# A spectral mix and a gated MLP on one core: the last down products of half 0 moved among the chains of half 1, row additions of half 0 alternating with half 1's rows, six fewer stored low parts

## Chip, cores and metric

One NeuronCore of one Trainium2 chip. The metric is the device time in microseconds of the kernel; three runs of the kernel before took 1344.32, 1346.24 and 1347.97 us, median 1346.24.

## What is computed

```python
g = sigmoid((x * gate_w).sum(-1, keepdims=True))
a = irfft2(rfft2(x) * (w_r + 1j * w_i), s=(S, D))     # S = 2048 tokens, D = 576
h = gelu(xB @ w_gate) * (xB @ w_up)                   # 576 -> 4608; here xB is A_x
b = h @ w_down                                        # 4608 -> 576
return g * a + (1 - g) * b
```

All in float32. The two branches share x. A float32 operand is kept as a high part rounded to 12 bits and a low part, the rest; a product takes three matmuls: high by high, low by high, high by low.

## The kernel before

**TensorE's programme.** The MLP sets the order. The tokens are two halves of 1024, p = 0 and 1, and a half runs over all 36 column blocks of the hidden layer, two at a time (18 pairs i). A step is numbered j = 36p + 2i, so step NT = 36 is the first of half 1. The first FIRST[p] pairs (3 and 7) are done by `normal`: for each of two token tiles tb, `hidden` runs a chain of 14 matmuls (128x512, `chain`) for the gate, one for the up weights, then gelu and the product, and splits the result into a buffer hb, hx, ext or part of gub. The other pairs are done by `products`: a block of seven products in place of eight (a11, a12, s2, s3, s1, a22, s4; n = 0 to 6), each two runs of seven matmuls (`seven`), from sums and differences of the weights (`prep`) and of the tokens (kept in til, xhi, xlo). Results wait in a list `pend`; `down` pops one: 12 matmuls of 128x288 (L909) into one of two PSUM banks pdn, evicted by ScalarE into one of four buffers stg (L941), and added to the output in DRAM, yd, by a DMA that accumulates, issued on GpSimd's queue, here Pool (L922).

**The other engines' order.** Every engine works strictly in the order in which the program issues to it. `gap()` is called twice in a chain, once after a run of seven, once after a down product; it counts, and issues what has come due: `at(n, fn)` runs fn n gaps later, `aux` holds one thing for each gap, `seq` a chain of steps with their distances, and `due` forces the rest of one when its result is needed. What is left of VectorE's time goes to a generator, `spectral`, by a credit: a matmul adds RATE times its time, an operation of the MLP subtracts its cost, and the spectral work (transforms along the rows in the tile rows, along the columns in til) continues while the credit is above zero.

**Between the halves.** In the last block of half 0, `leave(n)` loads the weights of step NT (early, in tmp) and the tokens of half 1 (rows), makes the hi and lo tokens of tile 0, and at n = 5 the high part of step NT's weights and the first of four loads til<-away (L1334), due 1, 6, 18 and 26 gaps later, for the column transforms. At n = 6 it issues the load of step NT+1 (L777, L778, into low) and queues the tokens of tile 1. Then six down products run (two of hb and hx, four of ext and gub), with the loads and copies of further weights between them (`prep_gu`, `prep_dn`: ScalarE copies the high part, VectorE subtracts, `lower` at L802), and then the first chain of half 1, step 36.

**The rows back.** `inverse_rows(h)` spreads half h's spectrum over rows (L545, L548, ScalarE L240), runs the row transforms, and adds each of the eight row tiles, scaled by the gate (L648 on ScalarE for odd t of half 0, else L650 on VectorE), to yd by an accumulating DMA (L651). A place for the scaled tile is one of three (part of gub, two spare), in turn; in half 1 four more in tmp. Half 1's spectrum lies in DRAM, spilt[0] and spilt[1], and passes through tmp (L636, L625).

**Low parts.** `lows`: for j of 14 to 35, the low part of w_down is stored to DRAM in half 0 (L805, SyncE) and loaded in half 1 (L798, Pool), so that VectorE need not subtract again.

Of the kernel before, what the change touches and what calls it, by code (L numbers as in the profile page):

```python
# [15 lines left out]
P = 128  # L16
S = 2048
D = 576
# [157 lines left out]
def _build(nc, tc, a):  # L176
    with ExitStack() as ctx:
# [376 lines left out]
        def waits(n):  # L554
            for _ in range(n):
                yield None
# [47 lines left out]
        def inverse_rows(h):  # L604
            pl.memset(rows.rearrange("p (c k) -> p c k", c=2)[:, :, 8 * KF:], 0.0)
            if h == 0:
                for e in range(2):
                    nc.sync.dma_start(spilt[e], til[:, 4 * SW * (2 + e):4 * SW * (3 + e)])
                fourth = [ext[:, 0:TB], ext[:, TB:2 * TB], xraw[:, 1]]
                for i in range(3):  # L610
                    nc.sync.dma_start(fourth[i], four_d[:, TB * i:TB * (i + 1)])
                T = til[:, 0:8 * SW].rearrange("p (t c k) -> p t c k", t=8, c=2)
                yield from moved(lambda t, c: (spread(c, t), T[:, t, c, 0:KF]), range(7, -1, -1))
                parts, tails = set_operands()
                for n in range(3):
                    nc.sync.dma_start(f(tails[3 + n]), kept[3 + n])
                for n in (1, 2, 0):
                    nc.sync.dma_start(f(parts[n].rearrange("p l t k -> p (l t k)")), kept[n][:, 0:2048])
                    nc.sync.dma_start(f(tails[n]), kept[n][:, 2048:])
                ops["ready"] = 1  # L620
                yield from inverse_stages()
            else:
                for e in range(2):
                    if e:
                        nc.sync.dma_start(tmp[:, 0:4 * SW], spilt[e])  # L625
                        yield from waits(9)
                    yield from moved(lambda t, c: (spread(c, t), batch[:, t - 4 * e, c, 0:KF]),
                                     range(4 * e, 4 * e + 4))
                yield from inverse_stages()
            R = rows.rearrange("p (k t) -> p t k", t=8)  # L630
            todo_t = list(range(8))
            while ops.get("phase") != 1:
                yield None
            places = [zb[0][:, 1920:1920 + D]] + spare
            if h == 0:
                at(2, lambda: nc.sync.dma_start(tmp[:, 0:4 * SW], spilt[0]))  # L636
            else:
                places += [tmp[:, D * i:D * (i + 1)] for i in range(4)]
            n = count[0]
            while todo_t:  # L640
                if count[0] >= n:
                    t = min(todo_t, key=lambda t: abs(count[0] - added[8 * h + t] - 11)) if h else todo_t[0]
                    todo_t.remove(t)
                    u = 8 * h + t
                    o = places.pop(0)
                    places.append(o)
                    if h == 0 and t % 2:
                        act.activation(o, R[:, t, 0:D], AF.Copy, scale=gs[:, u:u + 1])  # L648
                    else:
                        vec.tensor_scalar(o, R[:, t, 0:D], gs[:, u:u + 1], None, op0=ALU.mult)  # L650
                    at(2, lambda u=u, o=o: pl.dma_start(yd[u], o, accum_op=ALU.add))  # L651
                    n = count[0] + 1 + len(todo_t) % 2
                    yield 0.8
                else:
                    yield None
            yield from waits(3)
            ops["half"] = h + 1

        def load_rows(h):
            nc.sync.dma_start(rows[:, 0:8 * D], a["xn"][h])  # L660
# [129 lines left out]
            while q:  # L790
                q.pop(0)()

        lows = {j: dram.tile([P, D], F32, name=f"lo{j}", tag=f"lo{j}") for j in range(2 * FIRST[1], NT)}

        def lower(key, g, r, cost):
            j, kept_low = key[1], lows.get(key[1] % NT) if key[0] == "dn" else None
# [425 lines left out]
        def products(b, i):  # L1222
# [42 lines left out]
            for n, (name, nd) in enumerate(zip(("a11", "a12", "s2", "s3", "s1", "a22", "s4"), downs)):  # L1265
                m = n + 3
                b.prep(i + m // 7, m % 7)
                if n == 0 and i > b.first:
                    b.load_d(i)
                if p and n in (3, 4):  # L1270
# [41 lines left out]
        def leave(n):  # L1312
            nonlocal til

            if n == 0:
                assert ops["kept"]
                load_w(NT)
                for k in range(KT):
                    nc.sync.dma_start(rows[:, TB * k:TB * (k + 1)], a["xt"][1][:, k, 0:TB])
            if n == 2:  # L1320
                for k in range(KT):
                    aux.append(lambda k=k: prep_x(0, k, rows[:, TB * k:TB * (k + 1)]))
            if n == 1:
                for k in range(KT):
                    nc.sync.dma_start(rows[:, TB * (KT + k):TB * (KT + k + 1)], a["xt"][1][:, k, TB:2 * TB])
            if n == 5:
                z = BLOCKS[0][2]
                gub[z] = mk(f"gub{z}", [2560], F32R)
                prep_gu(NT)
            if n == 5:  # L1330
                til = mk("til", [16 * SW])
                there, here = (x.rearrange("p (e d k) -> p d e k", d=4, e=4) for x in (away, til))
                for d, n in enumerate((1, 6, 18, 26)):
                    at(n, lambda d=d: nc.sync.dma_start(here[:, d], there[:, d]))  # L1334
# [87 lines left out]
        def normal(p, i, tb, b):  # L1422

            j = 2 * (p * NBLK + i)
            first, last = p == 0 and i == 0, i == b.first - 1
            if last and tb == 0:
# [15 lines left out]
            def mid():  # L1442
                for _ in range(2):
                    if pend:
                        down(*pend.pop(0))

            if last and tb == 1:
                b.prep(b.first, 2, 4)
# [15 lines left out]
        for p in range(2):  # L1464
# [22 lines left out]


# [54 lines left out]
```

## Time and profile before

| | |
|---|---|
| median of three runs | 1346.24 us |
| the profiled execution | 1349.53 us, span 1347.8 us, mean granted TensorE clock 0.998 |
| TensorE busy | 1330.0 us |
| VectorE, ScalarE, GpSimd busy | 1141.1, 834.9, 274.9 us |
| DMA | 253.61 MB |
| TensorE idle in 640 to 700 us (60 us) | 4.57 us |
| in 900 to 1000 and 1000 to 1200 us | 1.42 and 1.83 us |

A row of a timeline gives the start and the duration in us, engine, line, operation and operands (out<-in, with partitions x elements), and in brackets the idle time ahead of it with what ended it. PE is TensorE, DVE VectorE, ACT ScalarE, SP SyncE; SPq marks the queue on which a DMA was issued. In a window's row stand its length, then the busy time of PE, weight loads, VectorE, ScalarE and GpSimd, the granted clock, the DMA share and GB/s. A row of the DMA issues gives the size and the median us from issue to landing. The span runs from the first to the last instruction; the time of an execution holds a little more.

### The profile page before, as it was taken

The numbers are of one execution on the slowest core, as the hardware profiler recorded it, in microseconds if no ns is written. First come the engines' busy times: TensorE is split into PE (matmuls) and PEld (weight loads), VectorE is DVE, ScalarE is ACT, GpSimd is POOL, SyncE is SP. The second block draws the span as 40 slices with busy tenths as digits, with TensorE's granted clock in tenths as the row PEclk, the third lists the DMA queues.
The fourth block names the chain that finished last, engine by engine and source line by source line (L and its number), as shares of the span: only waits on it lengthen the run. The fifth ranks groups of instructions, "written<-read, shape, count | busy, mean of one in ns | idle before, by whom it ended". The sixth has DMA issues, their size and how long they took to land.

```text
span 1347.8 us, 20213 instructions
## 1 busy us (share of the span) xinstructions
PE 1330.0 (99%) x7322; PEld 1173.3 (87%) x7322; DVE 1141.1 (85%) x1610; ACT 834.9 (62%) x1484; POOL 274.9 (20%) x350
## 2 busy tenths in 40 slices
PE   9999999999999999999899999999999999999998
PEld 7888888888888888888788888888888888888888
DVE  6999998789999988765688877879999948999964
ACT  5557656666665675786456666634675667666652
POOL 0021112212221221122201222111122232222241
PEclk9999999999999999999999999999999999999999
DMA  8464677787677679998979999767767799777797
GB/s 307 158 142 107 127 130 162 173 222 145 144 154 149 139 182 249 237 269 222 267 236 232 243 250 244 156 137 230 226 145 150 152 191 220 142 148 148 169 218 203
DMA packets 114755, 253.61 MB, mean 188 GB/s; under 512 B 13792, under 2 KB 24032, under 8 KB 112864
## 3 DMA queue, kind: packets, MB, share of 16 engines
q0 software_dynamic: 46880, 98.00, 44.2%
q1 hardware_dynamic: 67776, 154.34, 34.5%
q8 instruction: 57, 0.93, 0.3%
q14 instruction: 42, 0.34, 0.1%
HBM read 134.01 MB, written 111.13 MB: 182 GB/s over the span
## 4 chain that ended last, share of the span: by engine, by line
PE 84%; DVE 5%; DMA 3%; ACT 2%; issue 1%; POOL 0%; DVEq 0%; SPq 0%; ACTq 0%
PE pdn L909 29%; PE pgu L1216 18%; PE px L1216 17%; PE pgu L1218 3%; PE px L1218 3%; PE pgu L830 3%; PE pgu L831 3%; PE pgu L832 3%; PE px L302 1%; DMA low<-wd 1%; DMA yd<-spare 1%; PE px L830 1%; PE px L831 1%; PE px L832 1%; PE pgu L836 1%
## 5 line engine op out<-in xcount | busy, mean ns | idle before, releaser
L922 POOL DMA_DIRECT2D yd<-stg x264 | 225.2, 855 | 977.1 <-ACT stg L941 826.6
L941 ACT ACTIVATE stg<-pdn,omg 128x576 f32<-128x576 f32 x276 | 204.3, 741 | 307.9 <-PE pdn L909 197.7
L909 PE MATMUL pdn<-dn,hb 128*128 128x288 f32 x1644 | 241.6, 294 | 2.3 <-ACT stg L941 2.2
L909 PEld LDWEIGHTS pdn<-dn,hb 128*128 128x128 f32 x1644 | 231.7, 188 | 12.1 <-ACT stg L941 2.8
L240 ACT ACTIVATE gub<-low 128x512 fp32r<-128x512 f32 (+3 forms) x138 | 96.2, 697 | 37.9 <-DVE low L1193 19.5
L1216 PE MATMUL pgu<-xhi,gub 128*128 128x512 f32 x376 | 116.9, 392 | 0.9 <-ACT px L240 0.9
L1203 DVE TENSOR_TENSOR gub<-low,gub 128x768 fp32r<-128x768 f32 x114 | 108.5, 952 | 10.3 <-PE px L1218 6.5
L909 PE MATMUL pdn<-dn,ext 128*128 128x288 f32 x624 | 100.2, 296 | 5.1 <-ACT stg L941 4.6
L1216 PE MATMUL pgu<-til,gub 128*128 128x512 f32 x396 | 101.3, 391 | 0.0
L909 PEld LDWEIGHTS pdn<-dn,ext 128*128 128x128 f32 x624 | 91.6, 189 | 9.3 <-ACT stg L941 4.8
L909 PE MATMUL pdn<-dn,gub 128*128 128x288 f32 x624 | 99.6, 295 | 0.0
L909 PEld LDWEIGHTS pdn<-dn,gub 128*128 128x128 f32 x624 | 91.5, 189 | 3.6
L831 PE MATMUL pgu<-xhi,gub 128*128 128x512 f32 x240 | 93.8, 391 | 0.0
L830 PE MATMUL pgu<-xhi,gub 128*128 128x512 f32 x240 | 93.8, 391 | 0.0
L832 PE MATMUL pgu<-xlo,gub 128*128 128x512 f32 x240 | 93.6, 390 | 0.0
L909 PE MATMUL pdn<-dn,hx 128*128 128x288 f32 x540 | 86.2, 296 | 0.0
L1216 PEld LDWEIGHTS pgu<-til,gub 128*128 128x128 f32 x396 | 72.6, 188 | 13.7
L1216 PE MATMUL px<-til,gub 128*128 128x512 f32 x312 | 79.8, 391 | 0.0
L1216 PEld LDWEIGHTS pgu<-xhi,gub 128*128 128x128 f32 x376 | 67.9, 188 | 13.1 <-ACT px L240 1.3
L1216 PE MATMUL px<-xhi,gub 128*128 128x512 f32 x248 | 77.0, 392 | 0.0
L909 PEld LDWEIGHTS pdn<-dn,hx 128*128 128x128 f32 x540 | 76.6, 188 | 0.0
L1216 PE MATMUL pgu<-xlo,gub 128*128 128x512 f32 x188 | 73.2, 389 | 0.0
(259 smaller groups left out, 2935.6 us busy)
## 6 DMA issues: line engine op xcount, KB each, us to landing
yd<-stg POOLq DMA_DIRECT2D x264, 288.0 KB, 5.0
low<-ws SPq DMA_DIRECT2D x87, 384.0 KB, 5.3
gub<-wd SPq DMA_DIRECT2D x52, 288.0 KB, 4.3
low<-wgu SPq DMA_DIRECT2D x17, 640.0 KB, 6.4
rows<-col POOLq DMA_DIRECT2D x32, 256.0 KB, 5.5
gub<-ws SPq DMA_DIRECT2D x17, 384.0 KB, 4.8
lo<-dn SPq DMA_DIRECT2D x22, 288.0 KB, 3.3
dn<-lo POOLq DMA_DIRECT2D x22, 288.0 KB, 5.8
```

What stands on the lines that cost most here:

```text
L240: act.activation(o, i, AF.Copy)
L302: pe.matmul(v[al][:, :NK], c[:, al, q], two(x)[:, al], start=n == 0, stop=n == 2)
L830: pe.matmul(ps, w[:, 0, k, c], xhi[tb][:, k], start=k == 0, stop=False)
L831: pe.matmul(ps, w[:, 1, k, c], xhi[tb][:, k], start=False, stop=False)
L832: pe.matmul(ps, w[:, 0, k, c], xlo[tb][:, k], start=False, stop=False)
L836: pe.matmul(ps, w[:, 0, 4, c], xtl[tb], start=False, stop=False)
L909: pe.matmul(ps[half], h[:, l, c], d[:, q, half * HD:(half + 1) * HD], start=part == 0 and n == 0, stop=part == 1 and n == 2)
L922: pl.dma_start(yd[u], o, accum_op=ALU.add)
L941: at(n, lambda: put(u, lambda o: act.activation(o.rearrange("p (c k) -> p c k", c=2), v[:, :, 0:HD], AF.Copy, scale=omg[:, u:u + 1]), i == 0))
L1203: vec.tensor_tensor(w[:, 0:5:2], x, f(w[:, 1:4]), ALU.subtract)
L1216: pe.matmul(ps, l, x[:, t], start=first and t == 0 and q == 0, stop=False, skip_group_check=True)
L1218: pe.matmul(ps, w[:, 512 + P * s:512 + P * (s + 1)], xt, start=False, stop=True, skip_group_check=True)
```

## The change

1. After half 0, only two of the six down products run at once; the other four are popped in the first step of half 1, two after each of its two chains (`mid` given to `hidden`, then called). The load of step NT+1 moves from n = 6 to n = 5, ahead of the first til load; the copies of the weights of NT+1 and of w_down are put 1, 3 and 5 gaps after the block, further loads at 3 and 9, and the tokens of tile 1 go to `aux` behind the two down products.
2. `inverse_rows(0)` waits two gaps more before its transforms. Its eight additions are split: four, three gaps apart, while spilt[0] comes into tmp; then half 1's first four tiles are spread into rows (`back_again(0)`); then the other four, while spilt[1] comes; `inverse_rows(1)` spreads the rest. The additions of half 1 keep their distances.
3. `lows` ends at 29. For j of 30 to 35 half 0 stores nothing, and half 1 subtracts on VectorE.

```diff
+                yield from waits(2)
                 yield from inverse_stages()
             else:
-                for e in range(2):
-                    if e:
-                        nc.sync.dma_start(tmp[:, 0:4 * SW], spilt[e])
-                        yield from waits(9)
-                    yield from moved(lambda t, c: (spread(c, t), batch[:, t - 4 * e, c, 0:KF]),
-                                     range(4 * e, 4 * e + 4))
+                yield from back_again(1)
                 yield from inverse_stages()
...
             if h == 0:
+                n = count[0]
                 at(2, lambda: nc.sync.dma_start(tmp[:, 0:4 * SW], spilt[0]))
+                yield from adds(0, range(4), places)
+                while count[0] < n + 9:
+                    yield None
+                yield from back_again(0)
+                n = count[0]
+                at(1, lambda: nc.sync.dma_start(tmp[:, 0:4 * SW], spilt[1]))
+                yield from adds(0, range(4, 8), places)
+                while count[0] < n + 9:
+                    yield None
...
-                    n = count[0] + 1 + len(todo_t) % 2
+                    n = count[0] + (1 + len(todo_t) % 2 if h else 3)
...
-        lows = {j: dram.tile([P, D], F32, name=f"lo{j}", tag=f"lo{j}") for j in range(2 * FIRST[1], NT)}
+        lows = {j: dram.tile([P, D], F32, name=f"lo{j}", tag=f"lo{j}") for j in range(2 * FIRST[1], 30)}
...
-                    if p == 0:
+                    if p == 0 or (j + n - 4) % NT not in lows:
                         lower(("dn", j + n - 4), w, x, 0.76)
...
-            if n == 6:
                 load_w(NT + 1)
-                for k in (2, 3, 0, 1, 4):
-                    aux.append(lambda k=k: prep_x(1, k, rows[:, TB * (KT + k):TB * (KT + k + 1)]))
...
-            h0, key0 = hidden(j, tb, lambda: None)
+            turn = p and i == 0 and tb == 0
+            h0, key0 = hidden(j, tb, mid if turn else lambda: None)
+            if turn:
+                mid()
...
-                for n in range(6):
+                at(1, lambda: prep_gu(NT + 1))
+                at(3, lambda: [load_w(NT + 2), prep_dn(NT)])
+                at(5, lambda: prep_dn(NT + 1))
+                at(9, lambda: load_w(NT + 3))
+                for n in range(2):
                     down(*pend.pop(0))
-                    if n == 2:
-                        load_w(NT + 2)
-                        prep_dn(NT)
-                        prep_gu(NT + 1)
-                        prep_dn(NT + 1)
-                        at(6, lambda: load_w(NT + 3))
+                for k in range(KT):
+                    aux.append(lambda k=k: prep_x(1, k, rows[:, TB * (KT + k):TB * (KT + k + 1)]))
```

Between the halves, ScalarE's rows before. stg<-pdn are evictions, gub_70<-low and dn_75<-low copies of the weights of step NT+1, xhi_64 and xtl_68 tokens of tile 1:

```order
L941 ACTIVATE stg_88<-pdn,omg 128x576
L240 ACTIVATE xhi_64<-rows 128x512
L941 ACTIVATE stg_89<-pdn,omg 128x576
L1238 ACTIVATE xraw<-xraw 128x512
L240 ACTIVATE xhi_64<-rows 128x512
L941 ACTIVATE stg_86<-pdn,omg 128x576
L240 ACTIVATE xhi_64<-rows 128x512
L240 ACTIVATE dn_74<-tmp 128x576
L240 ACTIVATE gub_70<-low 128x1280
L240 ACTIVATE dn_75<-low 128x576
L941 ACTIVATE stg_87<-pdn,omg 128x576
```

The same place in the change (gl_83<-px is the gelu of the first chain of step 36):

```order
L952 ACTIVATE stg_88<-pdn,omg 128x576
L240 ACTIVATE gub_70<-low 128x1280
L952 ACTIVATE stg_89<-pdn,omg 128x576
L1249 ACTIVATE xraw<-xraw 128x512
L240 ACTIVATE dn_74<-tmp 128x576
L240 ACTIVATE xhi_64<-rows 128x512
L240 ACTIVATE hb_81<-xraw 128x512
L240 ACTIVATE xhi_64<-rows 128x512
L879 ACTIVATE gl_83<-px_5687 128x512
L952 ACTIVATE stg_86<-pdn,omg 128x576
L240 ACTIVATE dn_75<-low 128x576
```

The copy of step NT+1's weights moved from behind the third eviction to behind the first, and the gelu of a chain now stands among the evictions.

SyncE's queue at the same place, before (lo is a stored low part, low<-wgu and low<-wd first the load of step NT+1, then that of NT+2):

```order
L805 DMA lo_146<-dn_76 128x576
L1334 DMA til<-away 128x4x580
L805 DMA lo_147<-dn_77 128x576
L777 DMA low<-wgu 128x1280
L778 DMA low<-wd 128x576
L777 DMA low<-wgu 128x1280
```

and in the change:

```order
L788 DMA low<-wgu 128x1280
L789 DMA low<-wd 128x576
L1345 DMA til<-away 128x4x580
L788 DMA low<-wgu 128x1280
L789 DMA low<-wd 128x576
```

The two stores are gone and the load of step NT+1 stands ahead of the til load.

ScalarE at the additions of half 0, before (the scaled tiles are the rows with gs; rows<-tmp spreads half 1's spectrum):

```order
L240 ACTIVATE hb_82<-gl_83 128x512
L648 ACTIVATE spare_97<-rows,gs 128x576
L240 ACTIVATE xraw<-px_9701 128x512
L240 ACTIVATE gub_5639<-low 128x2x256
L1200 ACTIVATE gub_5639<-low,msk 128x256
L240 ACTIVATE xraw<-px_9702 128x512
L941 ACTIVATE stg_87<-pdn,omg 128x576
L240 ACTIVATE dn_76<-gub_8553 128x576
L648 ACTIVATE spare_96<-rows,gs 128x576
L240 ACTIVATE slot<-low 128x2x256
L1200 ACTIVATE slot<-low,msk 128x256
L941 ACTIVATE stg_88<-pdn,omg 128x576
```

and in the change:

```order
L240 ACTIVATE hb_82<-gl_83 128x512
L240 ACTIVATE xraw<-px_9686 128x512
L240 ACTIVATE gub_5628<-low 128x2x256
L1211 ACTIVATE gub_5628<-low,msk 128x256
L240 ACTIVATE xraw<-px_9687 128x512
L952 ACTIVATE stg_87<-pdn,omg 128x576
L240 ACTIVATE dn_76<-gub_8539 128x576
L240 ACTIVATE slot<-low 128x2x256
L1211 ACTIVATE slot<-low,msk 128x256
L661 ACTIVATE gub_8539<-rows,gs 128x576
L952 ACTIVATE stg_88<-pdn,omg 128x576
L240 ACTIVATE rows<-tmp 128x289 x3
```

In this stretch two scaled tiles became one, and the first spread of half 1 stands right behind an eviction, with more additions of half 0 after it.

More of the change, by code (lines that the diff above doesn't have):

```diff
@@ L620, in inverse_rows @@
                 ops["ready"] = 1
+                yield from waits(2)
                 yield from inverse_stages()
             else:
-                for e in range(2):
-                    if e:
-                        nc.sync.dma_start(tmp[:, 0:4 * SW], spilt[e])
-                        yield from waits(9)
-                    yield from moved(lambda t, c: (spread(c, t), batch[:, t - 4 * e, c, 0:KF]),
-                                     range(4 * e, 4 * e + 4))
+                yield from back_again(1)
                 yield from inverse_stages()
-            R = rows.rearrange("p (k t) -> p t k", t=8)
-            todo_t = list(range(8))
             while ops.get("phase") != 1:
@@ L635, in inverse_rows, with back_again, adds @@
             if h == 0:
+                n = count[0]
                 at(2, lambda: nc.sync.dma_start(tmp[:, 0:4 * SW], spilt[0]))
-            else:
-                places += [tmp[:, D * i:D * (i + 1)] for i in range(4)]
+                yield from adds(0, range(4), places)
[7 more added lines that the diff above has]
+                    yield None
+            else:
+                yield from adds(1, range(8), places + [tmp[:, D * i:D * (i + 1)] for i in range(4)])
+                yield from waits(3)
+            ops["half"] = h + 1
+        def back_again(e):
+            yield from moved(lambda t, c: (spread(c, t), batch[:, t - 4 * e, c, 0:KF]), range(4 * e, 4 * e + 4))
+        def adds(h, ts, places):
+            R = rows.rearrange("p (k t) -> p t k", t=8)
+            todo_t = list(ts)
             n = count[0]
@@ L655, in inverse_rows @@
                     yield None
-            yield from waits(3)
-            ops["half"] = h + 1
         def load_rows(h):
@@ L1269, in products @@
                     b.load_d(i)
-                if p and n in (3, 4):
+                if p and n in (3, 4) and (j + n - 3) % NT in lows:
                     lower(("dn", j + n - 3), dn[(j + n - 3) % 4], None, 0)
@@ L1425, in normal, with mid @@
             first, last = p == 0 and i == 0, i == b.first - 1
+            def mid():
+                for _ in range(2):
+                    if pend:
+                        down(*pend.pop(0))
             if last and tb == 0:
@@ L1440, in normal @@
                     b.prep(b.first, m, 2 * m)
[L1442 to L1445, printed above, removed]
             if last and tb == 1:
```

## The prediction

> **What bounds the kernel now.** I read the page first, then TensorE's waits, then the windows, then the timelines of the engines around each wait. The page's busy times, and the longest of TensorE's waits (total, times, longest, us):
>
> ```profile
> PE 1330.0 (99%) x7322; PEld 1173.3 (87%) x7322; DVE 1141.1 (85%) x1610; ACT 834.9 (62%) x1484; POOL 274.9 (20%) x350
> PE pdn L909 <- ACT stg L941: 6.7, 3, 4.6
> ```
>
> TensorE is the bound: 1330.0 of the 1347.8 us span. The change issues the same matmuls, so it can only win idle time, at most 17.8 us, and part of that is the start and the tail, which it does not touch. What counts is each single wait. The largest stands between the halves. TensorE there (start, duration, instruction, idle before in brackets):
>
> ```profile
> 636.39 0.69 PE L909 MATMUL pdn<-dn,ext 128*128 128x288 f32 x4
> 637.64 0.53 PE L909 MATMUL pdn<-dn,ext 128*128 128x288 f32 x2 [0.56 <-DVE ext L894]
> 646.71 1.81 PE L909 MATMUL pdn<-dn,ext 128*128 128x288 f32 x6 [4.57 <-ACT stg L941]
> 648.31 1.64 PE L909 MATMUL pdn<-dn,gub 128*128 128x288 f32 x6
> 649.75 0.49 PE L830 MATMUL px<-xhi,gub 128*128 128x512 f32 x1
> 653.07 0.39 PE L830 MATMUL px<-xhi,gub 128*128 128x512 f32 x1
> 656.24 0.39 PE L830 MATMUL pgu<-xhi,gub 128*128 128x512 f32 x1
> 659.41 3.33 PE L909 MATMUL pdn<-dn,hb 128*128 128x288 f32 x24
> 662.58 0.40 PE L830 MATMUL pgu<-xhi,gub 128*128 128x512 f32 x1
> ```
>
> ScalarE in the same stretch says why:
>
> ```profile
> 635.00 0.74 ACT L941 ACTIVATE stg<-pdn,omg 128x576 f32<-128x576 f32 x1 [1.82 <-PE pdn L909]
> 643.12 1.27 ACT L240 ACTIVATE gub<-low 128x1280 fp32r<-128x1280 f32 x1 [2.29 <-DMA low<-wgu]
> 645.34 0.68 ACT L240 ACTIVATE dn<-low 128x576 fp32r<-128x576 f32 x1 [0.95 <-DMA low<-wd]
> 645.93 0.72 ACT L941 ACTIVATE stg<-pdn,omg 128x576 f32<-128x576 f32 x1
> ```
>
> The eviction that TensorE needed stood behind two copies that waited for the weights of step NT+1. SyncE's queue issued those weights late:
>
> ```profile
> 628.63 0.53 SPq L1334 DMA_DIRECT2D til<-away  x1
> 630.02 0.43 SPq L777 DMA_DIRECT2D low<-wgu  x1
> ```
>
> **The transition: 7.2 us.** From 636.39 to the first matmul of step 37, that is NT+1, at 656.24 pass 19.85 us. The work in it is four down products and two chains. Two down products take 3.17 us (659.41 to 662.58), a chain takes 3.17 us (653.07 to 656.24), so 4 x 3.17 = 12.68 us. The other 7.17 us are the waits of 0.56 and 4.57, about 1.45 us in which the next down product ran slowly (646.71 to 649.75 is 3.04 for 1.59), and the rest. The new order puts a chain of half 1 where the first two of those down products were. Are its operands there at 636.39? These rows say so:
>
> ```profile
> 620.97 0.95 DVE L1203 TENSOR_TENSOR gub<-low,gub 128x768 fp32r<-128x768 f32 x1
> 623.55 0.75 DVE L245 SCALAR_TENSOR_TENSOR xtl<-xtl,msk,rows 128x512 fp32r<-128x512 f32 x1
> 624.22 0.75 DVE L802 TENSOR_TENSOR dn<-gub,dn 128x576 fp32r<-128x576 f32 x1
> 632.73 1.48 DVE L802 TENSOR_TENSOR gub<-tmp,gub 128x1280 fp32r<-128x1280 f32 x1
> ```
>
> The weights of step 36 are split by 632.73 + 1.48 = 634.2, and the last of its tokens by 623.55 + 0.75 = 624.3. Chain, two down products, chain, two down products then end at 649.07. The low parts of ext, late by 0.56 us before, now have a whole chain more.
>
> The hidden condition is ScalarE. Its new order has the copy of step NT+1's weights right behind the eviction at 635.00, at 635.74, and the eviction for the second hb/hx product behind that. TensorE needs that bank at 636.39 + 3.17 + 1.59 = 641.15, so the weights must land by 641.15 - 0.72 - 1.27 = 639.2. The load now stands ahead of the first til load on SyncE's queue, so it no longer waits for TensorE's last use of til (628.63), nor for the stored low parts that stood between. It can go when the last reader of its place is done, 620.97 + 0.95 = 621.9. The same load took from 630.02 to 643.12, 13.1 us, behind a til load of 1160 KB; without that load ahead it lands by 635.0. So ScalarE finds it there. I take the whole 7.17; the ends are 2.6 (all of 4.57 stays) and 7.17.
>
> The weight of the clock gate, in sentences by itself. The granted clock of the stretch was below one, and 1.18 us of idle later left it whole:
>
> ```profile
> 640.00:660.00 20.00, 15.43 (x76) 13.52 (x75) 9.51 (x13) 8.49 (x13) 5.60 (x8) 0.91 1.06 275
> 1100.00:1200.00 100.00, 98.82 (x546) 87.25 (x545) 89.07 (x110) 65.13 (x119) 25.66 (x32) 1.00 0.81 173
> ```
>
> The Trainium skill, TensorE: Matmul & The Clock Gate, Part 1 (what's actually happening), has the clock halved after an idle window of about 3.4 us and restored after about as long a busy one; by that the slow stretch would cost 1.7 us as an estimate instead of my 1.45, and this term would be 7.4. The trace agrees: 4.57 us of idle brought 0.91, and 1.18 us brought nothing. By the same rule a leftover wait under 3.4 us would cost only itself.
>
> **The first block of half 1: 1.2 us.** TensorE waits there twice; VectorE's and ScalarE's rows stand beside:
>
> ```profile
> 952.51 0.73 PE L1216 MATMUL pgu<-xhi,gub 128*128 128x512 f32 x2 [0.91 <-ACT px L240]
> 959.66 1.65 PE L1216 MATMUL px<-til,slot 128*128 128x512 f32 x6 [0.51 <-ACT xraw L240]
> 127.99 1.65 PE L1216 MATMUL px<-til,slot 128*128 128x512 f32 x6 [0.20 <-ACT xraw L240]
> 950.95 0.63 ACT L240 ACTIVATE slot<-low 128x512 fp32r<-128x512 f32 x1 [0.77 <-DVE low L1193]
> 947.77 1.40 DVE L502 TENSOR_TENSOR rows<-rows,msk 128x1200 f32<-128x1200 f32 x1
> ```
>
> ScalarE's copies waited for VectorE's differences, which stood behind long row operations. The two added turns put one butterfly half and one product of 1.40 us behind the differences, so ScalarE's 0.77 goes, and with it most of 0.91. At the second place I keep the 0.20 that half 0 has at the same place (127.99). 0.91 + 0.51 - 0.20 = 1.2; the ends are 0 and 1.42.
>
> **The row additions of half 0: 1.8 us.** Eight additions take turns in three places, and each place must be read by its DMA first. They followed each other every one or two gaps:
>
> ```profile
> 1094.44 1.64 PE L1216 MATMUL px<-til,slot 128*128 128x512 f32 x6 [0.65 <-ACT xraw L240]
> 1114.99 1.85 PE L909 MATMUL pdn<-dn,hb 128*128 128x288 f32 x12 [1.18 <-ACT stg L941]
> 1092.48 1.43 ACT L648 ACTIVATE gub<-rows,gs 128x576 f32<-128x576 f32 x1 [2.16 <-DMA yd<-gub]
> 1107.64 1.45 ACT L648 ACTIVATE spare<-rows,gs 128x576 f32<-128x576 f32 x1 [4.92 <-DMA yd<-spare]
> 1112.57 1.89 ACT L240 ACTIVATE rows<-tmp 128x289 f32<-128x289 f32 x3
> ...
> yd<-spare POOLq DMA_DIRECT2D x3, 288.0 KB, 6.8
> ```
>
> Now three gaps lie between them. Three gaps are one product and a down product, 3.17 + 1.59 = 4.8 us, so a place comes back after three additions, 14.3 us, and its DMA lands in 6.8. ScalarE has no such wait left, and the 0.65 + 1.18 = 1.83 go. What stands in for them is the second load of half 1's rows, which now must land inside nine gaps, 14.3 us:
>
> ```profile
> til<-away SPq DMA_DIRECT2D x2, 1160.0 KB, 14.9
> ...
> tmp<-spilt SPq DMA_DIRECT2D x1, 1160.0 KB, 8.6
> ...
> tmp<-spilt SPq DMA_DIRECT2D x1, 1160.0 KB, 6.7
> ```
>
> The loads of spilt, here from the DMA issues of 1076 to 1100 and of 1110 to 1118, took 8.6 and 6.7 us; the first row, from 600 to 640, is a load of the same size at the transition. ScalarE's three moves, which free the buffer, take 1.9 us of the fourteen, so 14.3 - 1.9 - 8.6 = 3.8 us are left. The ends are 1.83 and minus 2.5 us (14.9 - 12.4), if the load took those 14.9 us.
>
> **Six low parts: 0.** For 36 - 30 = 6 columns a store and a load of 288 KB go, and VectorE gets six subtractions of 0.75 us (the row at 624.22), 4.5 us, in the last three blocks. VectorE is nearly full there, but TensorE does not wait:
>
> ```profile
> 1200.00:1300.00 100.00, 100.00 (x561) 88.87 (x560) 91.33 (x133) 63.85 (x120) 27.83 (x35) 1.00 0.81 176
> ```
>
> Each subtraction is charged to the spectral work, which yields as much. Half 0 computes all its low parts this way, and by its timeline TensorE has no wait there between 127.99 and 637.64. If that cover is gone, up to 4.5 us come back; I take 0.
>
> **Sum.** 7.17 + 1.2 + 1.83 = 10.2. The profiled execution took 1349.53 us, so 1339.3 in its terms; it lies 3.3 above the median of the runs, 1346.24, and against that median I forecast 1336.0.
>
> **Rivals.**
> - The weights of NT+1 land late all the same, at 643 as before. ScalarE then holds the bank 3.9 us and the clock falls: 10.2 - 3.9 - 1.4 = 4.9 gained, 1341.3. For it: the DMA share of 1.06 at 640 to 660. Against: 17 us from 621.9 to 639.2, for a load that took 13.1. Chance 0.08.
> - The row additions lose their 1.8 to the second load: 1337.8 (only the 1.8 lost) to 1340.3 (2.5 lost as well). For it: the thin 3.8 us. Against: 6.7 measured at the same place. Chance 0.14.
> - VectorE becomes the bound: it is full in much of half 1, it loses the idle of the transition as time to catch up, and gets 4.5 us more. Gains of 10.2 would shrink to 0 to 5, 1341 to 1346. Against: its spectral work is rationed by TensorE's own time. Chance 0.09.
> - Slower: half 1's rows are done so late that TensorE stands before the last block's end, where all spectral work is drained. The last scaling was at 1296.35, the loads that need it at 1322.63:
>
> ```profile
> 1296.35 0.82 DVE L650 TENSOR_SCALAR tmp<-rows,gs 128x576 f32<-128x576 f32 x1
> 1322.63 9.18 SPq L961 DMA_DIRECT2D stg<-yd  x4
> ```
>
> That leaves 25 us. Beyond it each microsecond counts whole: 40 us late gives 1336.0 + 1.8 + 15 = 1353. Against: in the new order the last row addition on the Pool queue has eight evictions' DMAs behind it, where six were. Chance 0.05.
> - The change doing nothing is excluded by the new order itself.
>
> **How the numbers follow.** The forecast has 0.64. The range is 1334 (the lowest run lies 1.9 under the median) to 1343, which takes in the first two rivals and part of the third: about 0.83. What a measurement here can tell from no change is about 0.3%, 4 us: faster means under 1342.2, slower over 1350.3. Faster: 0.64 + 0.14 and half of the first rival = 0.82. Slower 0.05, same 0.13.
>
> **What would show it.** In the new profile: no idle of TensorE over 0.3 us between 630 and 660 and no granted clock under 1.00 there; step 37 starting 7 us earlier; ScalarE's copy of step NT+1 without a DMA wait; no wait of ScalarE or VectorE for yd; waits under 0.3 us in half 1's first block. A wait of the row moves for tmp<-spilt, or one of TensorE for a low part after 1180, would make me wrong, as would idle before the last block's end.

## The result, and the profile after

The changed kernel takes **1338.55 us** (median of 6 runs, 1337.83 to 1338.71); the kernel before, run on the same chip, 1346.89 us (6 runs, 1344.32 to 1348.63). The ratio is 0.9937, with a 95% interval of 0.9925 to 0.9950: 8.3 us gained, where 10.2 were forecast. The time lies inside the range of 1334 to 1343, 2.6 us above the predicted 1336.0. Two spreads belong to the result: 0.9 us between executions of the changed kernel, 4.3 between those of the kernel before.

The profiled execution took 1338.61 us (span 1336.8). The engines' busy times, and then three of TensorE's waits (total, times, longest):

```profile
PE 1327.8 (99%) x7322; PEld 1172.7 (88%) x7322; DVE 1145.6 (86%) x1616; ACT 835.0 (62%) x1484; POOL 274.4 (21%) x344
```

```profile
PE pdn L920 <- DVE hb L905: 1.0, 1, 1.0
PE px L1227 <- ACT xraw L240: 0.4, 2, 0.2
PE pdn L920 <- ACT stg L952: 0.2, 1, 0.2
```

The 6.7 us for stg have shrunk to 0.2, and of the waits for xraw (1.4 before) two of 0.2 are left. The wait of 1.0 for hb is new, but it stands at 31 us, in the start, where it comes and goes between executions (0.42 in e7, 0.72 in e12, none in e2). TensorE at the transition, and below it ScalarE and SyncE's queue (til<-away is the til load, which some of the expectations call the stash's return):

```profile
636.54 0.39 PE L841 MATMUL px<-xhi,gub 128*128 128x512 f32 x1
639.74 0.95 PE L920 MATMUL pdn<-dn,ext 128*128 128x288 f32 x6
642.90 0.40 PE L841 MATMUL px<-xhi,gub 128*128 128x512 f32 x1
646.11 0.95 PE L920 MATMUL pdn<-dn,ext 128*128 128x288 f32 x6
649.27 0.40 PE L841 MATMUL pgu<-xhi,gub 128*128 128x512 f32 x1
```

```profile
635.15 0.74 ACT L952 ACTIVATE stg<-pdn,omg 128x576 f32<-128x576 f32 x1 [1.82 <-PE pdn L920]
635.79 1.26 ACT L240 ACTIVATE gub<-low 128x1280 fp32r<-128x1280 f32 x1
636.95 0.73 ACT L952 ACTIVATE stg<-pdn,omg 128x576 f32<-128x576 f32 x1
```

```profile
622.13 0.33 SPq L788 DMA_DIRECT2D low<-wgu  x1
628.78 0.54 SPq L1345 DMA_DIRECT2D til<-away  x1
```

Chain, two down products, chain, two down products, no bracket: from 636.54 to step 37 at 649.27 pass 12.73 us, the pure work of the prediction (12.68). The load of step NT+1 left at 622.13, ahead of the til load, and the copy at 635.79 has no DMA wait. The windows (columns as before) show the clock whole:

```profile
640.00:660.00 20.00, 20.00 (x123) 18.25 (x122) 15.75 (x24) 9.56 (x15) 7.32 (x10) 1.00 1.08 297
1100.00:1200.00 100.00, 100.00 (x556) 88.67 (x555) 93.33 (x122) 67.92 (x125) 27.07 (x34) 1.00 0.79 172
1200.00:1300.00 100.00, 100.00 (x565) 89.17 (x564) 88.53 (x120) 60.31 (x108) 29.15 (x32) 1.00 0.85 172
```

TensorE is busy for all of each stretch. In the row additions ScalarE no longer waits for yd, and its moves do not wait for the second load of spilt, which took 8.4 us:

```profile
1092.29 1.38 ACT L661 ACTIVATE gub<-rows,gs 128x576 f32<-128x576 f32 x1
1102.28 1.45 ACT L661 ACTIVATE spare<-rows,gs 128x576 f32<-128x576 f32 x1
1114.32 1.95 ACT L240 ACTIVATE rows<-tmp 128x289 f32<-128x289 f32 x3
```

```profile
tmp<-spilt SPq DMA_DIRECT2D x1, 1160.0 KB, 8.4
```

One of the signs that the prediction named did appear: VectorE waited once for yd, and TensorE did not wait behind it.

```profile
1106.89 0.86 DVE L663 TENSOR_SCALAR gub<-rows,gs 128x576 f32<-128x576 f32 x1 [0.82 <-DMA yd<-gub]
```

**A ledger of the traces.** The same down products run in the same order in each kernel, so the start of one can be subtracted between two traces. Each row below is a profiled execution against that of the changed kernel (us); the columns are what it loses up to the transition (at 597 in the changed kernel's time), in the transition (to 892), in half 1's first block (to 969), and in the row additions (to 1128). Between 1128 and 1319 none of them loses or gains more than 0.05. (e11, whose loss lies behind 1319, is left to its own paragraph.)

| execution | start | transition | first block | row additions | end |
|---|---|---|---|---|---|
| before | -0.15 | 7.06 | 1.53 | 2.36 | 10.80 |
| before again (e1) | -0.95 | 6.71 | 1.57 | 2.06 | 9.39 |
| before, third (e12) | -0.78 | 5.21 | 1.54 | 4.31 | 10.28 |
| transition only (e2) | -0.60 | 0.04 | 1.53 | 1.90 | 2.87 |
| rows only (e3) | -1.54 | 2.19 | -0.02 | 0.00 | 0.63 |
| low parts only (e4) | -0.20 | 2.21 | 1.56 | 3.07 | 6.64 |
| early load only (e5) | 1.01 | 2.20 | 1.53 | 1.63 | 6.37 |
| late load (e6) | -1.05 | 0.89 | -0.02 | 0.00 | -0.18 |
| low parts kept (e7) | -0.60 | 0.03 | 0.00 | 0.00 | -0.57 |
| without two turns (e8) | -0.11 | 0.24 | 1.55 | 0.60 | 2.28 |
| late load, low parts stored (e9) | -0.66 | 1.03 | 0.00 | 0.00 | 0.37 |
| dense additions (e10) | -0.22 | 0.00 | -0.02 | 3.62 | 3.38 |

The profiled pair thus differs by 10.8 us, near the forecast sum; the medians differ by 8.3. The start alone varies by 2.6 us between executions (-1.54 to 1.01), so a single pair of times says little. The experiments ask which column is smaller in a usual execution.

### The profile page after: what moved, and what is told of

It reads as the page before. It is cut to its first block, busy times and chain, and to the rows that moved or that the text cites. A ratio compares the mean times of both kernels' runs of the same rounds, so it can differ in the third digit from the quotient of the medians.

```text
span 1336.8 us, 20198 instructions
## 1 busy us (share of the span) xinstructions
PE 1327.8 (99%) x7322; PEld 1172.7 (88%) x7322; DVE 1145.6 (86%) x1616; ACT 835.0 (62%) x1484; POOL 274.4 (21%) x344
## 4 chain that ended last, share of the span: by engine, by line
PE 87%; DVE 4%; DMA 2%; ACT 2%; issue 1%; SPq 1%; DVEq 0%; ACTq 0%
PE pdn L920 31%; PE pgu L1227 19%; PE px L1227 18%; PE pgu L1229 3%; PE px L1229 3%; PE pgu L841 3%; PE pgu L842 3%; PE pgu L843 3%; PE px L842 1%; PE px L841 1%; DMA xraw<-til 1%; PE px L843 1%; PE px L302 1%; PE pgu L847 1%; PE pgu L848 1%
## 5 line engine op out<-in xcount | busy, mean ns | idle before, releaser
L920 PEld LDWEIGHTS pdn<-dn,hb 128*128 128x128 f32 x1644 | 231.7, 188 | 10.8 <-DVE hb L905 1.2
```

What stands on the lines that cost most here:

```text
L920: pe.matmul(ps[half], h[:, l, c], d[:, q, half * HD:(half + 1) * HD], start=part == 0 and n == 0, stop=part == 1 and n == 2)
```

## The experiments

The first four ran on one chip beside 35 runs of the kernel before (median 1347.35), e5 to e8 beside 11 (1349.01), e9 to e12 beside 11 (1347.43). Losses against the changed kernel are taken from its 1338.55.

**e1, before again.** No edit.

> The kernel before, unchanged, with a second profile. The sum of the prediction (10.2 us) was read in one profiled execution that took 1349.53 us, 2.6 above the median of 1346.89; the change brought 8.3 us in the medians. Theory V (the waits vary): most waits that the change removes hang on the landing of a load, so they differ from one execution to the next, and the profiled one had more of them than usual. By V a second profile shows the span about 2 us shorter, at one of the same places: the transition (19.85 us from 636.39 to 656.24, of which 7.17 not work), the first block of half 1 (1.42 us of waits) or the row additions (1.83). Theory S (a term of the sum is too large, whatever the execution): the same waits to 0.3 us, and the missing 1.9 us come back as work somewhere in the changed kernel. Ratio 1.000 by both.

Measured: 1346.81 us, ratio 0.9993 (0.9980 to 1.0006). TensorE, ScalarE, and a window of the transition:

```profile
644.12 1.81 PE L909 MATMUL pdn<-dn,ext 128*128 128x288 f32 x6 [2.79 <-ACT stg L941]
```

```profile
640.52 1.27 ACT L240 ACTIVATE gub<-low 128x1280 fp32r<-128x1280 f32 x1 [0.49 <-DMA low<-wgu]
```

```profile
646.00:648.00 2.00, 2.00 (x8) 1.83 (x8) 1.68 (x3) 0.52 (x2) 0.89 (x1) 0.50 1.03 358
```

The weights landed at 640.52, not 643.12. The wait is 1.8 us shorter, but the clock stayed at 0.50 longer, and the transition takes 19.35 us for 19.85. So the wait does vary, as theory V has it, but the sum that V expected to shrink by about 2 us is nearly the same in this one look (9.39 for 10.80, of which 0.80 is the start).

**e2, the transition only.** Before, with the new order of the transition and the early load, from the diff shown above, and nothing of the rest.

> Before, with the reordered transition alone (two last down products among half 1's chains, the load of step NT+1 ahead of the stash's return). As predicted: minus 7.2 us, about 1339.7, ratio 0.9947. If the transition of a usual execution holds less than the profiled one, 5.3 us: 1341.6, ratio 0.9961. If it is the six low parts that cost 1.9 us: 1339.7. TensorE without a wait over 0.3 us between 630 and 660, and with the first block's waits (0.91, 0.51) and those of the row additions (0.65, 1.18) still there in some measure.

Measured: 1343.09 us, ratio 0.9971 (0.9960 to 0.9981), 2.6 to 5.4 us gained. The predicted 7.2 lie outside. Yet in the trace the transition is at its work alone (12.74 us), and the other waits are there:

```profile
945.04 0.73 PE L1216 MATMUL pgu<-xhi,gub 128*128 128x512 f32 x2 [0.91 <-ACT px L240]
952.19 1.65 PE L1216 MATMUL px<-til,slot 128*128 128x512 f32 x6 [0.51 <-ACT xraw L240]
1107.08 1.86 PE L909 MATMUL pdn<-dn,hb 128*128 128x288 f32 x12 [1.35 <-ACT stg L941]
```

Nothing was left to be won there; so a usual execution of the kernel before loses less at this place than the profiled one.

**e3, the rows only.** Before, with the two added turns and the alternating row additions.

> Before, with the two added turns and the row additions of half 0 in alternation with half 1's rows alone. As predicted: minus 1.2 and 1.8, 3.0 us, about 1343.9, ratio 0.9977. If these waits vary and are mostly smaller than in the one profile: minus 1.1, 1345.8, ratio 0.9992. The transition's waits (4.57 on stg, 0.56 on ext) stay in both. If the second load of half 1's rows came too late: a wait for tmp<-spilt and no gain, ratio 1.000.

Measured: 1343.88 us (1339.36 to 1346.37), ratio 0.9973 (0.9961 to 0.9985): 3.5 us, as predicted (3.0). Its transition has the old order, and this was the short one:

```profile
641.85 1.06 PE L920 MATMUL pdn<-dn,ext 128*128 128x288 f32 x6 [1.11 <-ACT stg L952]
```

The load had landed before ScalarE came to it, though both stores of low parts stood ahead of it on the queue. These 1.11 us, and 0.56 for ext ahead of them, are the idle time that the old order has when nothing is late; the clock stayed whole, and the transition took 14.92 us. This execution was the quickest of its twelve.

**e4, the low parts only.** Before, with these edits:

```diff
-        lows = {j: ... for j in range(2 * FIRST[1], NT)}
+        lows = {j: ... for j in range(2 * FIRST[1], 30)}
-                if p and n in (3, 4):
+                if p and n in (3, 4) and (j + n - 3) % NT in lows:
-                    if p == 0:
+                    if p == 0 or (j + n - 4) % NT not in lows:
```

> Before, with the six stored low parts given up alone. As predicted: 0, ratio 1.000, VectorE with 4.5 us more of subtractions and TensorE with no new wait after 1180. If the six subtractions do cost TensorE: plus 1.9 us, ratio 1.0014, and the other two parts then make the whole 10.2. Should the freed store and load help the transfers: minus up to 0.5 us.

Measured: 1344.51 us (1342.78 to 1345.83), ratio 0.9979 (0.9967 to 0.9991). Neither 0 nor a loss: 2.8 us gained. TensorE and SyncE's queue:

```profile
643.20 1.06 PE L909 MATMUL pdn<-dn,ext 128*128 128x288 f32 x6 [1.11 <-ACT stg L941]
```

```profile
628.59 0.54 SPq L1334 DMA_DIRECT2D til<-away  x1
629.25 0.63 SPq L777 DMA_DIRECT2D low<-wgu  x1
```

In the kernel before two stores of low parts (625.00 and 629.55 in its trace) stood on this queue ahead of the load. Without them it leaves at 629.25 for 630.02, lands before ScalarE's copy at 640.69, and the transition is the short one, 14.92 us. One trace is weak evidence here, since e3 had the short one with the stores in place; the stronger is that the mean granted clock was 0.999 or more in all eleven runs of e4, and down to 0.995 in the runs of the kernel before beside them.

**e5, the early load only.** Before, with

```diff
-            if n == 6:
-                load_w(NT + 1)
+                load_w(NT + 1)
+            if n == 6:
```

> Before, with the load of step NT+1's weights one group earlier on SyncE's queue, ahead of the stash's first return, and nothing else moved. So far the unchanged order has shown two transitions: 14.92 us with the granted clock at 1.00 (waits 0.56 and 1.11), and 19.35 to 19.85 us with the clock halved for some microseconds (waits 0.56 and 2.79 to 4.57), by the time at which the load lands. Theory V (the transition's term is the mean of the two): the early load always gives the short one, 14.9 us, clock 1.00 in nearly all executions: about minus 2.4, ratio 0.9982, and the rest of the reordering is worth 14.92 - 12.73 = 2.2. Theory O (the order of the products is what counts): ratio 1.000, the wait on stg stays at 2.8 or more.

Measured: 1344.55 us (1343.54 to 1346.72), ratio 0.9974 (0.9962 to 0.9987). The load leaves at 626.61, and the transition takes 14.91 us:

```profile
644.42 1.06 PE L909 MATMUL pdn<-dn,ext 128*128 128x288 f32 x6 [1.11 <-ACT stg L941]
```

Theory O falls. Two unlike edits (e4, e5) lead to the same transition and the same time, 1344.5, so both mend one thing: the lateness of this load. The gain beside its own runs of the kernel before is 4.5 us where 2.4 were expected; those runs were slower (1349.01) than the ones beside the result.

**e6, the changed kernel with the late load.**

```diff
                 back[0] = count[0] + 14
+            if n == 6:
                 load_w(NT + 1)
```

> The changed kernel with the load of step NT+1 put back behind the stash's first return. As the prediction has it, ScalarE's copy then holds the eviction that TensorE needs at 641.15: a load that lands between 639.3 and 643 gives 0 to 3.9 us of idle, and the clock halved in some of the executions. Theory V: plus 1 to 5 us, with a spread of several microseconds between executions, ratio to the kernel before 0.995 to 0.997, and DMA waits on low before that copy. Theory O: no change against the changed kernel, 0.9937.

Measured: 1338.63 us (1338.21 to 1339.49), ratio 0.9927 (0.9914 to 0.9939). ScalarE, and TensorE:

```profile
639.11 1.27 ACT L240 ACTIVATE gub<-low 128x1280 fp32r<-128x1280 f32 x1 [4.28 <-DMA low<-wgu]
```

```profile
641.07 1.06 PE L920 MATMUL pdn<-dn,ext 128*128 128x288 f32 x6 [0.64 <-ACT stg L952]
```

The DMA wait of the copy came as expected, the loss of 1 to 5 us did not. With the stores gone the load lands at 639.1. This execution runs 0.9 us ahead of the kernel before, so the limit of 639.2 that the prediction computed is 638.3 here: the load is 0.8 late, TensorE idles 0.64, and the transition loses 0.89 in the ledger. The clock stays whole, and the median shows nothing of it. My expectation had left out that the stores were still missing here.

**e9, late load and stored low parts.** As e6, with the three lines of e4 undone.

> The changed kernel with both again: the six low parts stored, and the load of step NT+1 behind the stash's first return and behind two of those stores, as before the change. With the late load alone the copy of the weights ran at 639.11 and TensorE idled 0.64 us. Theory V: with the stores ahead the load lands between 639 and 643 as in the kernel before, so ScalarE's copy holds the eviction that TensorE needs: 0.6 to 4 us of idle, in some executions with the clock halved: plus 1 to 5 us, 1339.5 to 1343.5, spread of several microseconds. Rival (the new order alone suffices, wherever the load is): 1338.6, spread under 1.5.

Measured: 1341.15 us, ratio 0.9957 (0.9941 to 0.9974). The six runs fall into 1339.11 to 1339.81 at a mean granted clock of 1.000 and 1342.49 to 1343.16 at 0.998 to 0.999. The profile caught one of the first kind:

```profile
641.60 1.06 PE L920 MATMUL pdn<-dn,ext 128*128 128x288 f32 x6 [0.78 <-ACT stg L952]
```

So, as far as six runs tell, the new order alone does not suffice. It needs the load early or the stores gone: each alone mends it (e7 below, and e6). That the slower kind lost its 3 us at the transition is inferred from their lower clock; none of them was profiled.

**e7, the changed kernel with the six low parts stored again.**

> The changed kernel with the six low parts stored and loaded again as before. Giving them up alone brought 2.8 us. Theory V (it brings that only by clearing the way for the load of step NT+1, whose place on the queue was behind two of those stores): here the load is already early, so at most 0.3 us are lost, 1338.6 to 1338.9, ratio 0.9937 to 0.9940. Rival (the six parts are worth 2.8 us by themselves, by less traffic or a freer SyncE queue): plus 2.8, about 1341.4, ratio 0.996.

Measured: 1338.21 us (1338.00 to 1338.78), ratio 0.9924 (0.9909 to 0.9938): nothing lost. The low parts are worth 2.8 us alone and nothing beside the early load; the prediction's 0 holds for the change as a whole. Whether the stores delay a load behind them by their place on the queue or by their bytes, no run separates.

**e8, without the two turns.**

```diff
-                yield from waits(2)
                 yield from inverse_stages()
```

> The changed kernel without the two turns put in ahead of half 1's spectral work. As predicted, the waits of half 1's first block come back (0.91 and 0.51 for 0.20): plus 1.2 us, 1339.8, ratio 0.9946. Rival (the spectral work running two turns earlier gives them back later, since VectorE is nearly full): 0, ratio 0.9937.

Measured: 1340.72 us (1340.63 to 1340.93), ratio 0.9941 (0.9929 to 0.9954), 2.1 us above e6 beside it. The first block's waits are back, and a small one later:

```profile
945.74 0.73 PE L1226 MATMUL pgu<-xhi,gub 128*128 128x512 f32 x2 [0.93 <-ACT px L240]
952.88 1.65 PE L1226 MATMUL px<-til,slot 128*128 128x512 f32 x6 [0.51 <-ACT xraw L240]
1114.46 0.73 PE L1226 MATMUL px<-xhi,gub 128*128 128x512 f32 x2 [0.31 <-ACT pgu L240]
```

By the ledger 1.55 in the first block, and 0.60 at the additions, which come two turns earlier.

**e10, dense additions.**

```diff
-                    n = count[0] + (1 + len(todo_t) % 2 if h else 3)
+                    n = count[0] + (1 + len(todo_t) % 2)
```

> The changed kernel with the row additions of half 0 again one or two gaps apart instead of three. As predicted: the places come back too early for their DMAs, ScalarE waits for yd again, and TensorE with it: plus 1.6 to 3.1 us (what the additions cost in five profiles of the old arrangement), 1340.2 to 1341.7, ratio 0.9950 to 0.9960. Rival (what counts is that four additions, not eight, stand in a row): 0, ratio 0.9937.

Measured: 1341.96 us, ratio 0.9957 (0.9942 to 0.9973), 3.4 us lost. ScalarE waits for yd again, TensorE behind it, and the clock follows:

```profile
1110.50 1.32 ACT L661 ACTIVATE spare<-rows,gs 128x576 f32<-128x576 f32 x1 [2.82 <-DMA yd<-spare]
```

```profile
1112.36 0.74 PE L1227 MATMUL px<-xhi,gub 128*128 128x512 f32 x2 [1.76 <-ACT pgu L240]
```

```profile
1114.00:1116.00 2.00, 2.00 (x6) 1.56 (x5) 2.00 (x5) 2.00 (x5) 1.26 (x2) 0.50 1.10 205
```

The three gaps between additions are what gives; four in a row instead of eight gives nothing by itself.

**e11, half 1's additions later.** In front of half 1's additions:

```diff
+                yield from waits(30)
                 yield from adds(1, range(8), places + ...)
```

> The changed kernel with half 1's row additions held back by 30 more gaps, 48 us. It tests the slower rival: 25 us of slack were read before the last block's end. As predicted, what goes beyond the slack counts whole: plus about 23 us, about 1361, ratio 1.011. Rival (the spectral work drains beside the last products, its lateness hides): plus 0 to 5.

Measured: 1358.53 us, ratio 1.0083 (1.0066 to 1.0101): 20.0 us above the changed kernel. The slower rival's mechanism is real. The 30 gaps moved the last scaling by 36 us, not the 48 expected (why is open). VectorE's last scaling, SyncE's load of yd behind it, and TensorE:

```profile
1321.66 0.72 DVE L664 TENSOR_SCALAR gub<-rows,gs 128x576 f32<-128x576 f32 x1
```

```profile
1335.82 1.75 SPq L973 DMA_DIRECT2D low<-yd  x4
```

```profile
1339.93 1.81 PE L921 MATMUL pdn<-dn,ext 128*128 128x288 f32 x6 [18.37 <-DVE low L984]
```

The clock was at 0.50 until 1345.9, so the first 6 us of work behind the wait cost about 3 more, an estimate from the clock.

**e12, before, a third look.** No edit.

> The kernel before once more, for the time of its transition in a third execution. Theory V: it is one of the two, 14.9 us at a granted clock of 1.00 or 19.3 to 19.9 us with a stretch near 0.5; nothing between. A smooth spread (16 to 18 us) would speak against the halved clock as what separates them.

Measured: 1349.03 us in its one run; a transition of 17.94 us, between the two. The expectation fails in that. TensorE and a window there, and a second place in the same execution:

```profile
644.05 1.07 PE L909 MATMUL pdn<-dn,ext 128*128 128x288 f32 x6 [2.53 <-ACT stg L941]
...
1112.96 3.12 PE L909 MATMUL pdn<-dn,hb 128*128 128x288 f32 x12 [2.00 <-ACT stg L941]
```

```profile
646.00:648.00 2.00, 2.00 (x6) 1.61 (x6) 1.74 (x3) 0.93 (x2) 1.28 (x2) 0.50 1.04 338
648.00:650.00 2.00, 2.00 (x8) 1.56 (x7) 2.00 (x3) 0.00 (x0) 1.97 (x4) 0.77 1.10 283
```

ScalarE waited 0.24 us for low<-wgu and 0.96 for low<-wd ahead of its two copies, so here most of the lateness is that of the second part of the load. The clock is halved here too, but for about half as long as in e1. The halved clock separates the transitions, but its length varies as well.

## Why the prediction held, and where it was off

- **The transition: the mechanism was right, and this is the term whose size was off.** Step 37 was computed for 649.07 - 636.39 = 12.68 us behind the last hx product and came 12.73 behind it; the load was expected at 621.9 and left at 622.13; the copy found its weights. What was wrong is the sentence "I take the whole 7.17" together with "so 1339.3 in its terms; [...] and against that median I forecast 1336.0": a wait that ends with the landing of a load was read in one execution and taken off the median of all. The transition of the old order loses 2.2 us when the load is in time (e3, e4, e5), and 5.2 to 7.1 when it is late and the clock halves (before, e1, e12). How often it is late the times say: e4 and e5, where the profile shows the load in time, run at 1344.5. The kernel before beside the result ran at 1346.89, 2.4 us more, so I estimate 2.2 + 2.4 = 4.6 us for the transition of its median execution, not 7.17. The 1346.89 and the 1344.5 come from different groups of runs. Each edit beside its own runs of the kernel before (1347.35, 1349.01) gives 2.2 + 2.8 = 5.0 by e4 and 2.2 + 4.5 = 6.7 by e5, and e2 takes the whole term away for 4.3. All are below 7.17, but the size is known only as 4.3 to 6.7. The changed kernel and those that differ from it in nothing that matters (e6, e7) stayed at 1338.2 to 1338.6; against the 1349.01 the gain was 10.4 to 10.8 us, so whether 10.2 was too much hangs on which runs of the kernel before one takes.
- **The first block: 1.2 predicted, 1.53 measured**, in every execution of the old arrangement alike. I had counted the brackets (0.91 + 0.51 - 0.20 = 1.22); where the other 0.3 sit I have not settled. By e8 the two turns are worth 0.6 more at the additions.
- **The row additions: 1.83 predicted, 2.36 in the same execution**, and 1.63 to 4.31 in the six of the old arrangement (median 2.2): these waits hang on the landing of yd. In e12 one of 2.00 us halved the clock too.
- **The six low parts: 0 predicted**, 0 in company (e7), 2.8 alone (e4). I had named the stored low parts that stood ahead of the load, but priced their removal by VectorE's work alone; what they cost was the lateness of the load behind them. The 4.5 us of subtractions cost nothing: TensorE is busy for 100.00 us of 1200 to 1300.
- **The sum** in the profiled pair is 7.06 + 1.53 + 2.36 - 0.15 (the start) = 10.8 for the 10.2 forecast. For the medians one part can be checked: with the load in time the ledger gives 2.2 + 1.5 + 2.2 = 5.9, and e4 and e5 ran 5.95 above the changed kernel. The other 2.4 of the 8.3 are put down to the late load and not measured by themselves. That the forecast came as near as it did is in part luck: the first block and the row additions gave more than predicted, 0.3 and some 0.4 us, and the transition less.
- **The rivals.** The chances of the range do not add up: the forecast and the first two rivals alone make 0.64 + 0.08 + 0.14 = 0.86, where "about 0.83" stands for these and part of the third. Late weights: not in the changed kernel, but made by e9, with 2.6 us in the median for the forecast 5.3 (3.9 and 1.4). A late second load of spilt: it took 8.4 us and nothing waited. VectorE as the bound: it is busy for 93.33 of 100 us at 1100 to 1200, TensorE for 100.00.
- **The rival of the drain.** The mechanism is shown by e11, the slack of 25 us was too large. It was read off two rows that do not bound it. The scaling at 1296.35 is the seventh of eight, and the loads at 1322.63 are the second group that needs them; the last scaling of the kernel before, and the first group, are these:

```profile
1300.50 0.78 DVE L650 TENSOR_SCALAR gub<-rows,gs 128x576 f32<-128x576 f32 x1
1311.09 7.63 SPq L961 DMA_DIRECT2D low<-yd  x4
```

And landing, load and addition count too. From the last scaling (1321.66) to the matmul (1339.93) pass 18.3 us of these in e11. In the changed kernel the last scaling stands at 1285.55, and the matmul that idled in e11 at 1322.60. If the same 18.3 us lie between, which I estimate from e11 alone, its slack is 1322.6 - 18.3 - 1285.6 = 18.7 us.
- **The clock gate.** The prediction has, by the Trainium skill (TensorE: Matmul & The Clock Gate, Part 1, What's actually happening: the clock halves after an idle window of about 3.4 us), that a wait under 3.4 us costs only itself. The runs disagree: waits of 2.79, 2.53, 2.00 and 1.76 us each brought a stretch at 0.50. The measurement decides. The same page of the Trainium skill calls the window free-running. With that the traces agree: two falls in e12 lie 467.63 us apart, 137 times 3.413 (last section).

## What to carry to other kernels

A wait that ends with the landing of a transfer is not a number but a distribution: before it is taken off a median, look at a second and a third execution, or at the spread of the times (4.3 us before, 0.9 in the changed kernel; the early load alone, e5, still had 3.2). Ask of every DMA that a change removes what stands behind it on its issuing queue; two stores of 288 KB were worth 2.8 us that way and nothing once the load stood ahead of them. And count a slack from the last producer to the first engine that will stand, with the landing, load and arithmetic between, not to an issue.

## What the runs showed of the hardware

TensorE's granted clock was halved behind idle times far shorter than the 4.57 us of the first profile: 1.76 us did it in e10 and 2.00 in e12, while 1.65 us in e4 left it whole. TensorE in e4, and the window behind that wait:

```profile
1110.81 1.85 PE L909 MATMUL pdn<-dn,hb 128*128 128x288 f32 x12 [1.65 <-ACT stg L941]
```

```profile
1112.00:1114.00 2.00, 2.00 (x12) 1.74 (x12) 2.00 (x4) 1.72 (x4) 0.00 (x0) 1.00 1.04 314
```

Added up over its windows, the slow stretch lasted 3.4 us in e10, 3.4 at each of the two places of e12, 3.4 in the first profile, and 6.8 in e1. There the slow clock behind a wait of 2.79 us cost some 2.8 us, more than behind the wait of 4.57 us in the first profile (1.45).

It also matters when the wait falls. The granted clock of e12 to a tenth of a microsecond (the third number from the right in each row):

```profile
645.40:645.50 0.10, 0.10 (x3) 0.10 (x3) 0.10 (x1) 0.10 (x1) 0.00 (x0) 1.00 1.14 277
645.50:645.60 0.10, 0.10 (x3) 0.10 (x2) 0.10 (x1) 0.10 (x2) 0.00 (x0) 0.51 1.26 300
1113.10:1113.20 0.10, 0.10 (x1) 0.10 (x2) 0.10 (x1) 0.10 (x1) 0.00 (x0) 0.64 0.78 115
```

It falls at 645.50 and at 1113.13. The 467.63 us between are 137 times 3.413, and the slow stretch of e11, 20.48 us from 1325.43, is 6 times 3.413. In each of the fourteen traces, all changes of the granted clock lie whole multiples of 3.413 us apart, as on a fixed grid. On that grid, the stretch just ahead of each fall holds 3.41 us of idle time in the first profile, 1.97 in e1, 1.97 and 2.00 in e12, and 1.76 in e10. The 1.65 us of e4 lie across a border (1109.95, counted back from its fall to half clock at 1342.05, 68 stretches later) as 0.79 and 0.86. Behind the start, the most that one stretch held without a fall is 1.44 us (e1, the wait that ends at 1113.57). In these few cases, then, more than 1.44 and at most 1.76 us of idle time within one stretch halve the clock for the next. In e1 the end of the wait, 0.82 us, falls into the first slow stretch, and a second followed; in the first profile 0.16 us did, and none followed. What idle time in a slow stretch prolongs it, these two cases do not tell.
